# Sixteen more exponential tiles on VectorE, with a second FFN activation buffer, FFN and output tiles spread over the span, and the last shift of these tiles done in place

## The chip, the cores and the metric

One core of a Trainium2 chip. The metric is the device time of one execution in microseconds, the median of several. All executions compared here are of the fast state. Ratios are the mean time of one kernel's fast runs over that of the other's in the same rounds, so they are not quite the ratio of the medians quoted beside them.

## The reference, cut to what matters

```python
xn = layernorm(x)                       # x: 2048 x 512
q, k, v = xn @ wq, xn @ wk, xn @ wv     # 32 query heads of 16, one key/value head
p = softmax(q @ k.T * 16 ** -0.5)       # 32 heads x 2048 x 2048 scores
attn = (p @ v) @ wo
ffn = gelu(xn @ w1 + b1) @ w2 + b2      # 1792 hidden columns, tanh form of gelu
return x + attn + ffn
```

Almost everything hangs on the 32 x 2048 x 2048 exponentials. They are cut into 2048 tiles of 128 keys by 512 queries of one head.

## The kernel before: the parts concerned

The kernel records every operation with its dependencies, and a list scheduler inside it fixes the order on each engine. ScalarE (ACT) does exponentials; VectorE (DVE) takes some tiles off it, the **D tiles**: an approximate exponential by integer arithmetic on the bit pattern, in five shifted versions, each multiplied with its own scaled V on PE. A string, `DTAB`, says for each unit of three tiles whether tile 0 or tile 2 is a D tile (`.`: none).

```python
def exp(u):                                   # one ACT instruction for the 2 or 3 other tiles
    exps.append(act(lambda e: e.activation(E[:, s0:s0 + na, :], bank(b0, na)..., ACT.Exp, ...)))
    for i, t in enumerate(ts):
        if is_d[t]: p1(t, 3 * x + i)

def p1(t, bk):                                # D tile, first step: out of PSUM
    dve(lambda e: e.tensor_scalar(Dt[:, KZ, s, :], bank(bk), ..., ALU.add, ALU.max), ...)

def close_batch():                            # up to KB = 3 D tiles
    for k in order:
        if k != KZ:                           # four shifts, each into a version of its own
            dve(lambda e, k=k: e.tensor_scalar(Dt[:, k, s0:s0 + n, :], Dt[:, KZ, s0:s0 + n, :],
                                               float(SPL_K[k]), None, ALU.add), ...)
        for t, s in batch:
            pv_mm(gg, j, 1 + k, kt, Dt[:, k, s, :].bitcast(bf), [("D", s, k)])
```

`Dt` has 5 versions of a ring of 8 slots. Beside this run, per block of 512 rows: 14 hidden tiles of the FFN (matmuls, eviction by DVE, GELU arithmetic on DVE with a tanh on ACT) into **one** buffer `ub`, and four output tiles that read `ub`. Where they stand in the stream of 683 units is set by constants: the output tiles of the previous block at units 3, 12, 21 and 30 of a block, its own hidden tiles from 40 to 165.

Of the kernel before, what the change touches and what calls it, by code (L numbers as in the profile page):

```python
# [10 lines left out]
P = 128  # L11
# [27 lines left out]
NE_ND_KB = (25, 8, 3)  # L39
LA = 34  # L40
LB = 105
LY = 9
LP = 121
LS = 107
# [6 lines left out]
DTAB = "...00.20.0022.00.2...202202.22..0.200220..220..0.02.222002.20...2200220.2.0.2220.0...200000..002002.2.00..200220..00.200.0000....02.220.22.0220.02...2.22200022.0.2..220..20200220.20.20.220....22.200.2222.020020...2220.222.0222.0.020......2.2..0..020202....0220.20..0022.02.0...22..2220.2020.22.20...0.020020002...0020...02.00..0002202.022....222.2222.2222.0000..222.0.0222.022.200....00000.2020.00.02.2...22202.2.22.0000.000...2.2200.22..22.20.0...2.2.2.002..020020....220.2200.002.22.000....000020.2200.22200...02202.2.2002..2022...222220..0.2222.0020..22.00002.02.222020....20222...0202..0..2...220....2000.2.0.22....2.2.2.00..2.002020...0.00.2202.02000.00...20022.02.00.202000...."  # L51
# [7 lines left out]
YS = 9  # L59
HA = 40  # L60
HB = 165
# [365 lines left out]
def bass_parallel_sum__grouped_kv_mqa__dense_activation_gelu__prompt_kernel(  # L427
# [27 lines left out]
    NPR = 5  # L455
    NV = 1 + len(SPL_K)
    KZ = SPL_K.index(0)
    GAM = 128.0 / LN2 * 0.25
# [3 lines left out]
    with ExitStack() as es:  # L462
# [4 lines left out]
        ub = sb([P, FT, TBW], bf, "ub")  # L467
        xn = ub[:, 0:8, :]
        xnT = sb([P, DT, S], bf, "xnT")
        wvk = sb([P, DT, 2 * Dh], bf, "wvk")  # L470
        wkp = sb([P, DT, 4, 32], bf, "wkp")
        wq_sb = sb([P, DT, D], bf, "wq_sb")
        wqp = sb([P, DT, HG, 32], bf, "wqp")
# [31 lines left out]
        scr = sb([P, D], bf, "scr")  # L505
# [4 lines left out]
        ksq = sb([P, NT, Dh], f32, "ksq")  # L510
# [5 lines left out]
        Vf = sb([P, NT, Dh], f32, "Vf")  # L516
# [6 lines left out]
        Dt = sb([P, len(SPL_K), ND, TBW], i16, "Dt")  # L523
# [7 lines left out]
        oTp = sb([P, NPR, TBW], bf, "oTp")  # L531
# [41 lines left out]
        def dma(eng, o, i, stream, r=(), w=(), lat=2.2, allow=1.0, **kw):  # L573
            return add(eng, lambda e: e.dma_start(o, i), r, w, dma=stream, occ=0.7, lat=lat, allow=allow, **kw)
# [29 lines left out]
        dve(lambda e: e.memset(wkp[:], 0.0), w=["wkp"], n=256, due=0.0)  # L604
        dve(lambda e: e.memset(wqp[:], 0.0), w=["wqp"], n=512, due=0.1)
# [14 lines left out]
        for v, c in enumerate((1.0,) + SPL_C):  # L620
            setup(lambda e, v=v, c=c: e.memset(V1[:, v, :, Dh:Dh + 1], c), r=["V1"], w=["V1"], due=11.0)
        setup(lambda e: e.memset(sel8[:], 0.0), w=["sel8"], occ=0.3, due=12.0)
# [16 lines left out]
        def ln_batch(ts, how):  # L639
# [4 lines left out]
            if how == "a":  # L644
                for ti in ts:
                    act(lambda e, ti=ti: e.activation(scr[:], x_sb[:, ti, :], ACT.Identity, accum_out=sm[:, ti:ti + 1]),
                        r=[("x", ti)], w=["scr", ("sm", ti)], n=TBW + 250, due=land(ti))
                setup(lambda e: e.tensor_scalar(mean[:, sl], sm[:, sl], 1.0 / D, None, ALU.mult),
                      r=[("sm", ti) for ti in ts], w=mk, occ=0.2)
                setup(lambda e: e.tensor_scalar(nm[:, sl], sm[:, sl], -1.0 / D, None, ALU.mult),  # L650
                      r=[("sm", ti) for ti in ts], w=[("nm", ti) for ti in ts], occ=0.2)
                for ti in ts:
                    act(lambda e, ti=ti: e.activation(scr[:], x_sb[:, ti, :], ACT.Square, bias=nm[:, ti:ti + 1],
                                                      accum_out=sm[:, ti:ti + 1]),
                        r=[("x", ti), ("nm", ti)], w=["scr", ("sm", ti)], n=TBW + 250, due=land(ti))
                setup(lambda e: e.tensor_scalar(ve_b[:, sl], sm[:, sl], 1.0 / D, 1e-5, ALU.mult, ALU.add),
                      r=[("sm", ti) for ti in ts], w=[("ve", b)], occ=0.2)
            else:
                for ti in ts:
                    dve(lambda e, ti=ti: e.bn_stats(stats[:, ti, :], x_sb[:, ti, :]), r=[("x", ti)], w=[("st", ti)],  # L660
                        n=530, due=land(ti) + 1.0)
# [32 lines left out]
        def normed(ti):  # L694
            b, mean_ap = batch_of[ti]
            if XN_ENG[ti] == "d":
                dve(lambda e: e.tensor_scalar(xn[:, ti % 8, :], x_sb[:, ti, :], mean_ap, rstd[:, ti:ti + 1], ALU.subtract, ALU.mult),  # L697
                    r=[("x", ti), ("rstd", b), ("mv", b, ti)], w=[("u", ti % 8)], n=270, due=land(ti) + 2.0)
            else:
                act(lambda e: e.activation(xn[:, ti % 8, :], x_sb[:, ti, :], ACT.Identity, bias=nmr[:, ti:ti + 1],  # L700
                                           scale=rstd[:, ti:ti + 1]),
                    r=[("x", ti), ("rstd", b), ("nmr", b)], w=[("u", ti % 8)], n=TBW + 60, due=land(ti) + 2.0)

        def x_T(ts, bk, eng):
# [5 lines left out]
            for k, ti in enumerate(ts):  # L710
                for d in range(DT):
                    o = (d * n + k) * P
                    add("pe", lambda e, ti=ti, d=d, o=o: e.transpose(pT[:, o:o + P], xn[:, ti % 8, d * P:(d + 1) * P], ident[:]),  # L713
                        r=[("u", ti % 8), "ident"], w=[B(bk)], occ=0.085, due=land(ti) + 3.0)
# [95 lines left out]
        for v, c in enumerate(SPL_C):  # L810
            setup(lambda e, v=v, c=c: e.tensor_scalar(V1[:, 1 + v, :, 0:Dh], Vf[:], c, None, ALU.mult),
# [69 lines left out]
        def p1(t, bk):  # L881
            if not batch and dptr[0] + KB > ND:
# [4 lines left out]
            dve(lambda e: e.tensor_scalar(Dt[:, KZ, s, :], bank(bk), float(127 * 128) + SPL_D, SPL_MIN, ALU.add, ALU.max),  # L887
                w=[B(bk), ("D", s, KZ)], allow=P1_ALLOW, kind="p1")
# [7 lines left out]
        def close_batch():  # L896
            n = len(batch)
            s0 = batch[0][1]
            order = [KZ] + [k for k in range(len(SPL_K)) if k != KZ]
            for k in order:  # L900
                if k != KZ:
                    dve(lambda e, k=k: e.tensor_scalar(Dt[:, k, s0:s0 + n, :], Dt[:, KZ, s0:s0 + n, :], float(SPL_K[k]),  # L902
                                                       None, ALU.add),
                        r=[("D", s0 + i, KZ) for i in range(n)], w=[("D", s0 + i, k) for i in range(n)],
                        n=n * TBW, mode=4, allow=1.0, kind="post")
                for t, s in batch:
                    gg, kt, j = tile_of(t)
                    pv_mm(gg, j, 1 + k, kt, Dt[:, k, s, :].bitcast(bf), [("D", s, k)])
            del batch[:]

        onorm = {}

        def o_evac(gg):
# [20 lines left out]
            if h or end:  # L934
# [3 lines left out]
                                                r=keys, w=[("oTp", sl)], allow=3.0)  # L938
# [54 lines left out]

        def h_mm(tb, ft, ev=EV_ALLOW):
# [6 lines left out]
        def h_chain(tb, fts, al=3.0):  # L1001
# [3 lines left out]
            uu = ub[:, f0:f0 + n, :]  # L1005
            hk = [("h", s0 + i) for i in range(n)]
            uk = [("u", f) for f in fts]
# [8 lines left out]
        def y_mm(tb, i, start=True, stop=False, bk=7, fts=range(FT), al=1.5):  # L1016
            for ft in fts:
                mm4(bank(bk), ub[:, ft, i * P:(i + 1) * P], w2_sb[:, ft, :], start and ft == fts[0], stop and ft == fts[-1],
                   r=[("u", ft), "w2"], w=[B(bk)], allow=al)

        def wo_mm(tb, i, ps, start=False, bk=7, al=1.5):
            for n, p in enumerate(ps):
                pp = tb * NGR // 2 + p
                hs = [h for h in range(2) if 2 * pp + h < NTB * NGR - 1]
                assert all(2 * pp + h in onorm for h in hs)
# [6 lines left out]
        def store(tb, i):  # L1032
            ti = tb * 4 + i
            dma("sp", of[ti * P:(ti + 1) * P, :], x_sb[:, ti, :], f"d_o{i}", r=[("x", ti)], w=[("ob", i)])

        def out_tile(tb, i):
# [3 lines left out]
            ti = tb * 4 + i  # L1040
            dve(lambda e: e.tensor_tensor(x_sb[:, ti, :], pM, x_sb[:, ti, :], ALU.add), w=[("x", ti)] + M4, allow=EV_ALLOW)
            store(tb, i)

        xpy = x_sb[:, 0:8, :].rearrange("p t d -> p (t d)").bitcast(f32).rearrange("p (t d) -> p t d", d=D)

        def y_tile(tb, i):
            ti = tb * 4 + i
            y_mm(tb, i, al=YT_ALLOW[i])
            wo_mm(tb, i, range(FIN_G), al=YT_ALLOW[i])
            b2_mm(stop=i < 3, al=YT_ALLOW[i])  # L1050
            if i < 3:
                dve(lambda e: e.tensor_tensor(xpy[:, i, :], pM, x_sb[:, ti, :], ALU.add), r=[("x", ti)],
                    w=M4 + [("x", 2 * i), ("x", 2 * i + 1)], allow=EV_ALLOW)
            else:
                mm4(pM, ident, x_sb[:, ti, :], False, False, r=["ident", ("x", ti)], w=[B(7)], allow=YT_ALLOW[i])
# [22 lines left out]
        for tb in range(NTB):  # L1078
            u0 = tb * UPT
            if tb > 0:  # L1080
                for i in range(4):
                    at(u0 + 3 + (YS if tb < NTB - 1 else 9) * i, lambda tb=tb, i=i: out_tile(tb - 1, i), 0.6)
                q_at(tb, 3, u0 + Q3, (2, 3), (4, 5, 6, 7))
            a, b = (HA, HB) if tb < NTB - 1 else (LA, LB)
            if tb == 0:
                a = 18
            nf = FT if tb < NTB - 1 else FT - FIN_F
            for f0 in range(0, nf, 3):
                fts = list(range(f0, min(nf, f0 + 3)))
                for ft in fts:  # L1090
                    at(u0 + a + (b - a) * ft / FT, lambda tb=tb, ft=ft: h_mm(tb, ft), 0.6)
                at(u0 + a + (b - a) * fts[-1] / FT, lambda tb=tb, fts=fts: h_chain(tb, fts), len(fts) * 1.067 + 0.33)
# [3 lines left out]
            else:  # L1096
                for i in range(4):
                    at(u0 + LS + LY * i, lambda tb=tb, i=i: y_tile(tb, i), 0.6)
                fts = list(range(nf, FT))
                for ft in fts:  # L1100
                    at(u0 + LP + ft - nf, lambda tb=tb, ft=ft: h_mm(tb, ft), 0.6)
                if fts:
                    at(u0 + LP + len(fts), lambda tb=tb, fts=fts: h_chain(tb, fts, LAL), (len(fts) * 1.067 + 0.33) * LCO)
# [66 lines left out]
        for i in (0, 1, 3, 2):  # L1170
            ti = tb * 4 + i
            w = [(B(FB[i]), j) for j in range(4)] + ([B(FB[i])] if i < 3 else []) + [("x", ti)]
            if i < 3:
                dve(lambda e, i=i, ti=ti: e.tensor_tensor(x_sb[:, ti, :], bank(FB[i]), xpy[:, i, :], ALU.add),
                    r=[("x", 2 * i), ("x", 2 * i + 1)], w=w)
            else:
                act(lambda e, i=i, ti=ti: e.activation(x_sb[:, ti, :], bank(FB[i]), ACT.Copy), w=w)
            store(tb, i)
# [44 lines left out]
```

## Time and profile before

| | before |
|---|---|
| time, median | 797.58 us (796.94 to 798.07) |
| busy: PE, DVE, ACT | 767.0, 739.8, 774.0 us of a span of 795.8 |
| D tiles | 439 |
| start of first exponential, of last, end | 30.00, 785.36, 795.81 us |

The lines behind it stand in the prediction, with the measure that is used throughout: for ACT, the distance between the starts of successive instructions. 0.903 us for a two-tile and 1.330 for a three-tile exponential (medians in this trace: 0.904 and 1.330) are taken as the price without a wait; what is over that is called late, although the profile counts part of it as busy.

### The profile page before, as it was taken

How to read it: one execution, taken by the hardware profiler on the slowest of the kernel's cores; microseconds unless marked ns; L12 is line 12 of the kernel's file. 1: busy time of each engine (PE TensorE's matmuls, PEld its weight loads, DVE VectorE, ACT ScalarE, POOL GpSimd, SP SyncE). 2: the span in 40 equal slices, each digit the busy share in tenths (PEclk: the TensorE clock that was granted, in tenths of full speed). 3: DMA queues.
4: the chain of work that ended last, by engine and by line, in shares of the span. 5: the costliest groups of instructions: out<-in, count | busy, mean ns of one | idle time of the engine just before them, and what ended most of it. 6: DMA issues, size and time to landing. Idle time of an engine off the chain costs nothing.

```text
span 795.8 us, 20778 instructions
## 1 busy us (share of the span) xinstructions
PE 767.0 (96%) x8759; PEld 240.5 (30%) x8759; DVE 739.8 (93%) x1401; ACT 774.0 (97%) x734; POOL 20.8 (3%) x84
## 2 busy tenths in 40 slices
PE   6799999999999999999999999999999999999998
PEld 4323322232222323322232233322233233323222
DVE  8589999999998959999999889999999998999896
ACT  4899999999999999999999999999999999999995
POOL 6300000000000000000000000000000000000000
PEclk7899999999999999999999999999999999999999
DMA  9101100000000010001000001100001010000001
GB/s 312 41 9 30 23 15 16 17 21 13 12 22 23 23 29 16 17 15 22 17 13 24 20 19 23 22 16 16 19 12 22 24 22 23 16 9 16 16 9 35
DMA packets 30007, 21.17 MB, mean 27 GB/s; under 512 B 16353, under 2 KB 25434, under 8 KB 29914
## 3 DMA queue, kind: packets, MB, share of 16 engines
q1 hardware_dynamic: 28330, 19.28, 9.4%
q8 instruction: 69, 1.13, 0.6%
q10 hardware_dynamic: 1584, 0.56, 0.3%
q14 instruction: 24, 0.20, 0.1%
HBM read 10.98 MB, written 2.35 MB: 17 GB/s over the span
## 4 chain that ended last, share of the span: by engine, by line
ACT 92%; PE 5%; DVE 3%; DMA 0%; issue 0%; DVEq 0%
ACT E L870 88%; ACT ub L1012 3%; PE pAll L891 2%; PE pAll L851 1%; DVE stats L660 1%; PE pAll L567 1%; PE pAll L561 1%; DVE Dt L887 0%; DVE Dt L902 0%; DMA x_sb<-in_A_x_dram 0%; ACT xnT L718 0%; PE pAll L713 0%; ACT KT L732 0%; ACT ub L700 0%; DVE ub L697 0%
## 5 line engine op out<-in xcount | busy, mean ns | idle before, releaser
L870 ACT ACTIVATE E<-pAll 128x1024 bf16<-128x1024 f32 (+1 forms) x683 | 736.7, 1335 | 1.5 <-PE pAll L851 1.3
L891 PE MATMUL pAll<-Dt,V 128*32 128x512 bf16 x2195 | 390.0, 383 | 0.3
L887 DVE TENSOR_SCALAR Dt<-pAll 128x512 int16<-128x512 f32 x439 | 292.9, 680 | 28.9 <-PE pAll L851 28.3
L891 PE MATMUL pAll<-E,V 128*32 128x512 bf16 x1609 | 303.2, 387 | 1.4 <-DVE Of L915 1.2
L902 DVE TENSOR_SCALAR Dt<-Dt 128x1536 int16<-128x1536 int16 (+1 forms) x608 | 297.6, 533 | 0.9
L851 PE MATMUL pAll<-QT,KT 32*128 32x512 bf16 x2048 | 268.3, 386 | 15.0 <-ACT E L870 8.4
L851 PEld LDWEIGHTS pAll<-QT,KT 32*128 32x128 bf16 x2048 | 68.8, 91 | 290.4 <-ACT E L870 222.9
L891 PEld LDWEIGHTS pAll<-Dt,V 128*32 128x32 bf16 x2195 | 105.6, 94 | 107.0 <-issue 54.8
L567 PE MATMUL pAll<-xnT,w_sb 128*32 128x512 bf16 x896 | 128.1, 382 | 0.1
L567 PE MATMUL pAll<-w_sb,ub 128*32 128x512 bf16 x896 | 125.4, 382 | 0.0
L891 PEld LDWEIGHTS pAll<-E,V 128*32 128x32 bf16 x1609 | 70.7, 93 | 77.0 <-issue 59.1
L567 PE MATMUL pAll<-wop,oTp 128*32 128x512 bf16 x256 | 50.8, 381 | 0.0
L998 DVE TENSOR_SCALAR hb<-pAll,b1T 128x512 bf16<-128x512 f32 x56 | 41.5, 740 | 0.8 <-PE pAll L891 0.5
L567 PEld LDWEIGHTS pAll<-xnT,w_sb 128*32 128x32 bf16 x896 | 33.6, 95 | 24.1 <-issue 10.0
L567 PEld LDWEIGHTS pAll<-w_sb,ub 128*32 128x32 bf16 x896 | 32.1, 95 | 11.8 <-issue 5.2
L1184 PE MATMUL pAll<-xnT,zeros 128*32 128x512 bf16 x308 | 33.1, 383 | 0.0
L1012 ACT ACTIVATE ub<-ub 128x1536 bf16<-128x1536 bf16 (+1 forms) x20 | 32.1, 1606 | 0.0
L915 DVE COPY Of<-pAll 128x512 f32<-128x512 f32 x31 | 21.1, 680 | 5.0 <-PE pAll L567 4.1
L567 PE MATMUL pAll<-xnT,wq_sb 128*32 128x512 bf16 x256 | 20.5, 398 | 0.0
L1011 DVE TENSOR_TENSOR ub<-ub,hb 128x1536 bf16<-128x1536 bf16 (+1 forms) x20 | 17.9, 893 | 0.1
L1014 DVE TENSOR_TENSOR ub<-ub,hb 128x1536 bf16<-128x1536 bf16 (+1 forms) x20 | 17.9, 894 | 0.1
L1009 DVE TENSOR_TENSOR ub<-hb 128x1536 bf16<-128x1536 bf16 (+1 forms) x20 | 17.8, 892 | 0.1
(124 smaller groups left out, 242.7 us busy)
## 6 DMA issues: line engine op xcount, KB each, us to landing
OfP<-Of SPq DMA_DIRECT2D x124, 32.0 KB, 1.9
rbP<-rden_rows SPq DMA_DIRECT2D x124, 32.0 KB, 1.8
w_sb<-in_B_w_dram SPq DMA_DIRECT2D x2, 1792.0 KB, 13.5
x_sb<-in_A_x_dram SPq DMA_DIRECT2D x8, 256.0 KB, 6.1
out_dram<-x_sb SPq DMA_DIRECT2D x16, 128.0 KB, 1.7
QT<-qp SPq DMA_DIRECT2D x124, 16.0 KB, 1.8
wq_sb<-in_A_wq_dram ACTq DMA_DIRECT2D x1, 512.0 KB, 6.5
wop<-in_A_wo_dram SPq DMA_DIRECT2D x1, 512.0 KB, 16.3
```

The lines of the kernel that those rows point to most:

```text
L567: add("pe", lambda e, c=c, j=j: e.matmul(o[c, :], l[:, c], rh, start=start, stop=stop, tile_position=(0, 32 * j)), r, [(k, j) for k in w] ...
L851: ins = e.matmul(o, l, rh, start=True, stop=True, tile_position=(q0, 0))
L870: exps.append(act(lambda e: e.activation(E[:, s0:s0 + na, :], bank(b0, na).rearrange("p (a n) -> p a n", a=na), ACT.Exp, scale=LN2 / 128.0 ...
L887: dve(lambda e: e.tensor_scalar(Dt[:, KZ, s, :], bank(bk), float(127 * 128) + SPL_D, SPL_MIN, ALU.add, ALU.max), w=[B(bk), ("D", s, KZ)], ...
L891: add("pe", lambda e, a, b: e.matmul(pO[32 * j:32 * j + 32, :], V1[:, v, kt, :], rhs, start=a, stop=b, tile_position=(0, 32 * j)), r=r + [ ...
L902: dve(lambda e, k=k: e.tensor_scalar(Dt[:, k, s0:s0 + n, :], Dt[:, KZ, s0:s0 + n, :], float(SPL_K[k]), None, ALU.add), r=[("D", s0 + i, KZ ...
L915: dve(lambda e: e.tensor_copy(Of[:, i, :], pO), w=["O", ("Of", i)], allow=0.0)
L998: dve(lambda e: e.tensor_scalar(hb[:, ft % 6, :], pM, b1T[:, ft:ft + 1], None, ALU.add), r=["b1T"], w=M4 + [("h", ft % 6)], allow=ev)
L1011: dve(lambda e: e.tensor_tensor(uu, uu, hh, ALU.mult), r=uk + hk, w=uk, n=c, mode=2, allow=al)
L1012: act(lambda e: e.activation(uu, uu, ACT.Tanh, scale=GELU_K), r=uk, w=uk, n=c, allow=al - 0.5, kind="tanh")
L1014: dve(lambda e: e.tensor_tensor(uu, uu, hh, ALU.mult), r=uk + hk, w=uk, n=c, mode=2, allow=al)
L1184: pr.filler = lambda e, j, o: e.matmul((pO if o else pM)[32 * j:32 * j + 32, :], zeros[:, 0:32], xnT[:, 0, 0:TBW], start=not o, stop=not o ...
```

## The change

The intent is to give ACT fewer tiles and DVE more, which needs an evener load on DVE. Three parts make the room, and the fourth uses it:

- a second FFN activation buffer, laid over `x` (blocks alternate between `ub` and `x_sb`; the x rows that an output tile adds are loaded again from HBM);
- hidden and output tiles placed by two explicit lists that overlap;
- the last shift of a batch written over its first version, so that four versions suffice and the ring can be 12 instead of 8 (setup scratch moves into `oTp` for room);
- a new `DTAB` with 455 D tiles instead of 439.

Two small sizes change with them: the ring of exponentials `E` goes from 25 to 23 tile slots, and `oTp` from 5 to 6.

```diff
-NE_ND_KB = (25, 8, 3)
+NE_ND_KB = (23,12,3)
-DTAB = "...00.20.0022.00.2...202202.22..0.200220. [cut] "     # 439
+DTAB = "....0.2022200.2200...20.02002.20.02.0000. [cut] "     # 455
-YS = 9
-HA = 40
-HB = 165
+HP = ((18,160),(180,320),(330,470),(480,590))                       # hidden tiles, in units
+YP = ((174,213,252,291),(345,384,423,462),(516,537,558,579),(600,620,640,647))   # output tiles
+        ubs = (ub, x_sb)
-        Dt = sb([P, len(SPL_K), ND, TBW], i16, "Dt")
+        Dt = sb([P, len(SPL_K) - 1, ND, TBW], i16, "Dt")
 [cut: close_batch]
+                elif step:                                  # last shift
+                    b = 0
+                        dve(lambda e, k=k: e.tensor_scalar(Dt[:, 0, s0:s0 + n, :], Dt[:, 0, s0:s0 + n, :], ...
 [cut]
-            uu = ub[:, f0:f0 + n, :]
+            uu = ubs[tb % 2][:, f0:f0 + n, :]
+        def x_load(tb, i):
+            dma("sp", x_sb[:, 14 + i % 2, :], x_view[:, ti, :], ...)
```

## The prediction

> **What bounds the kernel now.** I read the page's busy shares first, then the chain that ended last, then the groups of instructions, then stretches of 100 us.
>
> ```profile
> PE 767.0 (96%) x8759; PEld 240.5 (30%) x8759; DVE 739.8 (93%) x1401; ACT 774.0 (97%) x734; POOL 20.8 (3%) x84
> ...
> ACT 92%; PE 5%; DVE 3%; DMA 0%; issue 0%; DVEq 0%
> ...
> L870 ACT ACTIVATE E<-pAll 128x1024 bf16<-128x1024 f32 (+1 forms) x683 | 736.7, 1335 | 1.5 <-PE pAll L851 1.3
> L887 DVE TENSOR_SCALAR Dt<-pAll 128x512 int16<-128x512 f32 x439 | 292.9, 680 | 28.9 <-PE pAll L851 28.3
> ```
>
> Three engines are over 90% busy, so the shares alone decide nothing. The chain decides: 92% of the span is ScalarE (ACT), and the exponentials waited only 1.5 us in all. VectorE (DVE) had 28.9 us of idle before the D tiles' first instruction, waiting for scores to appear: it was ahead of the others, not behind.
>
> The 2048 score tiles are handled three to a unit, 683 units. In each unit ACT exponentiates two or three tiles; the third may be a "D tile" that DVE turns into an approximate exponential by integer arithmetic (one step out of PSUM, then four shifts in SBUF on batches of up to three, each followed by a multiplication with V). The same groups with forms kept apart:
>
> ```profile
> L870 ACT ACTIVATE E<-pAll 128x1024 bf16<-128x1024 f32 x440 | 447.3, 1189 | 0.8 <-PE pAll L851 0.6
> L870 ACT ACTIVATE E<-pAll 128x1536 bf16<-128x1536 f32 x243 | 364.3, 1599 | 0.7 <-PE pAll L851 0.7
> L902 DVE TENSOR_SCALAR Dt<-Dt 128x1536 int16<-128x1536 int16 x548 | 277.4, 548 | 0.9
> L902 DVE TENSOR_SCALAR Dt<-Dt 128x1024 int16<-128x1024 int16 x52 | 18.9, 415 | 0.0
> L902 DVE TENSOR_SCALAR Dt<-Dt 128x512 int16<-128x512 int16 x8 | 1.8, 279 | 0.0
> ```
>
> The busy sums (447.3 + 364.3 = 811.6) exceed the 736.7 of the union, so consecutive instructions overlap and the mean duration is not the price. The price is the distance between successive starts in the trace. Its medians: two-tile exponential 0.904 us, three-tile 1.330, wide tanh 1.373; on DVE, D tile's first step 0.601, shift of three tiles 0.468, of two 0.335, of one 0.202. At undisturbed prices (0.903 and 1.330) the exponentials need 440 x 0.903 + 243 x 1.330 = 720.5 us. The starts before the next instruction sum to 733.4; about 3 us of the excess is the wait after the very last one, so ACT loses about 10 us of some 755 (from first exponential at 30.0 to last at 785.4). **ACT is full; only less work on it shortens the kernel.** Outside that stretch lie 30 us of prologue and 10.4 us of tail.
>
> ```profile
> 200.00:300.00 100.00, 98.64 (x1204) 29.46 (x1203) 87.95 (x169) 100.00 (x94) 0.00 (x0) 1.00 0.09 21
> 300.00:400.00 100.00, 98.49 (x1055) 30.13 (x1054) 98.86 (x185) 100.00 (x94) 0.00 (x0) 1.00 0.08 17
> 400.00:500.00 100.00, 99.47 (x1211) 30.29 (x1211) 92.21 (x179) 100.00 (x95) 0.00 (x0) 1.00 0.08 20
> 500.00:600.00 100.00, 97.39 (x1056) 29.48 (x1054) 99.01 (x180) 99.40 (x93) 0.00 (x0) 1.00 0.07 17
> ```
>
> Columns: stretch, then PE, PEld, DVE, ACT, POOL busy, granted clock, DMA share, GB/s. DVE alternates between 88 to 92% and 99%. The low stretches are where the output tiles of one block of 512 rows are computed (1211 matmuls against 1055) and no FFN activation is; the high ones are where the FFN hidden tiles and their GELU arithmetic run. There is one activation buffer, so a block's hidden tiles cannot be written until the previous block's output tiles have read theirs.
>
> **What the Trainium skill says.** "Perfetto Trace Analysis", section Optimizing Scalar/DVE Operations, puts ACT's busy overhead at about 51 ns with a PSUM operand and 93 ns on SBUF, and says the profiled latency is longer because its acknowledgement overlaps the next instruction. The trace agrees: 1024 elements at the 1.2 GHz of "ScalarE: Activation LUTs", Specifications, are 853 ns, plus 51 is 904; tanh on SBUF 1280 + 93 = 1373. For DVE the page gives 125 ns on PSUM; the trace's 601 ns less 512/0.96 GHz = 533 leaves only 68, so I use the trace. "VectorE: DVE Perf Modes", The perf-mode tier table, lets a 16-bit tensor_scalar in SBUF run at 4x; 1536/4/0.96 = 400, measured 468: agrees, and an in-place shift, with equal shapes and types, should cost the same. "Perfetto Trace Analysis", Optimization Strategy, recommends interleaving regimes with different limits, which is the intent here.
>
> **The change part by part.** I counted the instructions of both programs in their scheduled order.
>
> *D tiles moved from ACT to DVE: 439 becomes 455.* Two-tile exponentials go 440 to 456, three-tile 243 to 227. ACT: 16 x (1.330 - 0.903) = **-6.8 us**, all on the path. Tanh count and size are unchanged (16 wide, 4 narrow).
>
> *DVE gains.* First steps +16 x 0.60 = 9.6. Shifts of three tiles 548 to 564, +16 x 0.467 = 7.5; of two 52 to 48, -1.3; of one 8 to 32, +4.9 (161 batches for 152, with more small ones at group ends). Sum **+20.6 us**, beside ACT's work if it fits.
>
> *Does it fit?* At these prices (0.60 for other 512-column steps, 0.66 for hidden tile evictions, 0.866 and 0.466 for the wide GELU steps) DVE's work from the first D tile on is 706.6 us before and 726.6 after; ACT's exponentials and tanh are 746.3 before and 739.4 after. DVE over ACT: 94.7% to 98.3%. Cut in sixteen parts of 43 units, DVE/ACT was 79% at worst and 104% at most before; after, apart from the first part, it lies between 93 and 104%, and the running surplus never exceeds a few us. That evenness is what the second buffer and the spread of FFN and output tiles buy; by themselves they remove nothing from ACT.
>
> *PE.* Five multiplications for a D tile instead of one: 64 more. The trace starts these 32-row matmuls about 0.054 us apart when the four column groups are filled (estimate: 16 in a 0.86 us piece of the chain), so +3.5 us. But filler matmuls, which only occupy PE's gaps, fall from 308 to 212, so -5.2. PE keeps a small margin.
>
> *DMA.* The second buffer lies over x, so 16 reloads of x (128 KB each) are added, six units (some 6 us) before use. The stores of equal size land in 1.7 us at a DMA share of 7 to 10%. Zero on the path.
>
> *In-place last shift, ring of 12.* It frees one of five versions (5 x 8 = 40 tile slots become 4 x 12 = 48), and four full batches instead of two may be in flight. The new cost is a dependency: the in-place shift must wait until PE has read the unshifted tiles. In the scheduled order only 3 of 161 in-place shifts directly follow their own third shift; the median has 2.5 us of other DVE work between them, and 6.9 us since the batch's last first step. Estimate 0 to 3 us on DVE.
>
> *Sum.* 797.7 - 6.8 = 790.9. The trace's two-tile exponentials lose 28 ns each on average, the three-tile ones 2, so 16 more add 0.4. For a DVE without slack I add 0.3: **791.6**.
>
> **Rivals.** (a) *DVE becomes the bound.* Slack of 12.8 us at prices, plus ACT's own 10 us of losses, against DVE waits that were not mere slack: 5.0 us for finished attention sums, 3.9 for output tiles, perhaps 5 of the 28.9 before first steps. That is 14 of 23 us: fits, narrowly. Were half the 28.9 unavoidable, the end would come near 795. Against it: in 300 to 400 us DVE was already at 98.86% and ACT lost 1.0 us; in 200 to 300, with DVE at 87.95%, it lost 1.6. A full DVE did not slow ACT.
> (b) *The in-place shift waits on PE.* 161 batches by 0.2 us would be 32 us on DVE, more than its slack, and give about 800. The order of instructions speaks against it.
> (c) *Spreading the bursts removes ACT losses too.* If the 10 us of losses fell by a third, about 788. The losses are spread evenly (0.1 to 0.4 in nearly every 20 us), which looks like jitter of two-tile units, so I give it little.
> (d) *PE becomes the bound* where output tiles now share the stretch with hidden tiles: 798. The clock was 1.00 throughout and fillers remain.
>
> **Range and chances.** The floor is near 787 and needs (c) as well; (a) and (b) push up. Range 789 to 796. Faster by 2% would be below 781.8, twice the ACT saving: 0.01. Slower by 2% is above 813.7, needing a systematic stall: 0.02.
>
> **What would show it.** Right: 456 and 227 exponentials at 0.903 and 1.330 between starts, chain still about 92% ACT, DVE near 760 us busy (96%), its idle before first steps far below 28.9, an even DVE row, no wait on the reloads. Wrong: two-tile exponentials with a mean well above 0.93, a large DVE idle before the in-place shift, or scores waiting for DVE to free PSUM (29.2 us before).

## The result, and the profile after

789.04 us (788.29 to 790.68, four runs) against 797.58: 8.5 us less, ratio 0.9896 with a 95% interval of 0.9877 to 0.9915. It is a clear gain of 1%.

The page of the changed kernel, the lines that answer to those of the prediction (busy, the chain by engine, the two groups):

```profile
PE 759.7 (97%) x8727; PEld 235.3 (30%) x8727; DVE 756.6 (96%) x1453; ACT 767.0 (97%) x734; POOL 20.6 (3%) x84
...
ACT 96%; DVE 2%; PE 1%; DMA 0%; issue 0%; DVEq 0%
...
L883 ACT ACTIVATE E<-pAll 128x1024 bf16<-128x1024 f32 (+1 forms) x683 | 729.4, 1342 | 0.4 <-PE pAll L864 0.4
...
L900 DVE TENSOR_SCALAR Dt<-pAll 128x512 int16<-128x512 f32 x455 | 304.9, 681 | 8.1 <-PE pAll L864 7.2
```

ACT's share of the chain went up, from 92 to 96%, and PE's fell from 5 to 1%: that is a kernel closer to its one bound. DVE's idle before the D tiles' first step fell from 28.9 to 8.1 us; its spare time has been spent.

The forms of the exponential apart, and the shifts, of which L926 is the one in place:

```profile
L883 ACT ACTIVATE E<-pAll 128x1024 bf16<-128x1024 f32 x456 | 459.7, 1204 | 0.0
L883 ACT ACTIVATE E<-pAll 128x1536 bf16<-128x1536 f32 x227 | 339.9, 1619 | 0.4 <-PE pAll L864 0.4
...
L917 DVE TENSOR_SCALAR Dt<-Dt 128x1536 int16<-128x1536 int16 x423 | 218.2, 549 | 0.3
L926 DVE TENSOR_SCALAR Dt<-Dt 128x1536 int16<-128x1536 int16 x141 | 75.3, 544 | 0.2
```

The in-place shift cost DVE 0.2 us of waiting in all, and it is as fast as the others. The same stretches of 100 us (PE, PEld, DVE, ACT, POOL busy, clock, DMA share, GB/s):

```profile
200.00:300.00 100.00, 98.71 (x1157) 29.24 (x1152) 98.32 (x192) 100.00 (x97) 0.00 (x0) 1.00 0.09 23
300.00:400.00 100.00, 98.36 (x1125) 30.26 (x1123) 98.77 (x189) 100.00 (x95) 0.00 (x0) 1.00 0.09 22
400.00:500.00 100.00, 98.68 (x1151) 30.09 (x1146) 99.66 (x195) 100.00 (x95) 0.00 (x0) 1.00 0.09 21
500.00:600.00 100.00, 98.79 (x1137) 29.25 (x1132) 99.44 (x188) 100.00 (x96) 0.00 (x0) 1.00 0.10 22
```

DVE, 88 and 99% in turn before, is now at 98 to 100% throughout, and PE's matmuls are even too (1125 to 1157 per stretch, before 1055 to 1211). The 16 reloads of x landed in 2.1 us, and no engine's wait after the prologue names them.

Where the 9.2 us between the two profiled executions lie, from the starts of the first and the last exponential:

| us | before | changed | difference |
|---|---|---|---|
| start of the first exponential | 30.00 | 29.69 | -0.30 |
| first to last exponential | 755.36 | 747.37 | -7.99 |
| last exponential to the end | 10.45 | 9.55 | -0.90 |

The first line is less than what a repeat of the same kernel moves (0.48 us, below). The middle line is 1.2 us more than the 6.8 us that 16 cheaper units give, and the last line was not foreseen at all. The experiments had to explain both, and to show which parts of the change were needed.

### The profile page after: what moved, and what is told of

It reads as the page before. It is cut to its first block, busy times and chain, and to the rows that moved or that the text cites. A ratio compares the mean times of both kernels' runs of the same rounds, so it can differ in the third digit from the quotient of the medians.

```text
span 786.6 us, 20791 instructions
## 1 busy us (share of the span) xinstructions
PE 759.7 (97%) x8727; PEld 235.3 (30%) x8727; DVE 756.6 (96%) x1453; ACT 767.0 (97%) x734; POOL 20.6 (3%) x84
## 4 chain that ended last, share of the span: by engine, by line
ACT 96%; DVE 2%; PE 1%; DMA 0%; issue 0%; DVEq 0%
ACT E L883 92%; ACT ub L1038 2%; ACT x_sb L1038 2%; DVE stats L673 1%; PE pAll L570 1%; DMA x_sb<-in_A_x_dram 0%; ACT xnT L731 0%; PE pAll L726 0%; ACT KT L745 0%; ACT ub L713 0%; DVE ub L710 0%; DVE ub L1198 0%; DVE QT L772 0%; PE pAll L904 0%; PE pAll L576 0%
## 5 line engine op out<-in xcount | busy, mean ns | idle before, releaser
L883 ACT ACTIVATE E<-pAll 128x1024 bf16<-128x1024 f32 (+1 forms) x683 | 729.4, 1342 | 0.4 <-PE pAll L864 0.4
L904 PE MATMUL pAll<-Dt,V 128*32 128x512 bf16 x2275 | 388.6, 383 | 0.3
L900 DVE TENSOR_SCALAR Dt<-pAll 128x512 int16<-128x512 f32 x455 | 304.9, 681 | 8.1 <-PE pAll L864 7.2
L904 PE MATMUL pAll<-E,V 128*32 128x512 bf16 x1593 | 295.0, 387 | 0.8 <-DVE Of L938 0.3
L917 DVE TENSOR_SCALAR Dt<-Dt 128x1536 int16<-128x1536 int16 (+2 forms) x483 | 236.3, 526 | 0.3
L904 PEld LDWEIGHTS pAll<-Dt,V 128*32 128x32 bf16 x2275 | 103.9, 94 | 109.7 <-issue 58.7
L576 PE MATMUL pAll<-xnT,w_sb 128*32 128x512 bf16 x896 | 110.5, 382 | 0.2
L904 PEld LDWEIGHTS pAll<-E,V 128*32 128x32 bf16 x1593 | 68.7, 93 | 71.6 <-issue 55.4
L926 DVE TENSOR_SCALAR Dt<-Dt 128x1536 int16<-128x1536 int16 (+2 forms) x161 | 81.7, 521 | 0.2
L576 PE MATMUL pAll<-w_sb,ub 128*32 128x512 bf16 x448 | 58.6, 381 | 0.0
L576 PE MATMUL pAll<-w_sb,x_sb 128*32 128x512 bf16 x448 | 55.2, 382 | 0.0
L576 PE MATMUL pAll<-wop,oTp 128*32 128x512 bf16 x256 | 51.8, 382 | 0.0
L576 PEld LDWEIGHTS pAll<-xnT,w_sb 128*32 128x32 bf16 x896 | 29.0, 95 | 21.5 <-issue 10.9
L1208 PE MATMUL pAll<-xnT,zeros 128*32 128x512 bf16 x212 | 23.8, 383 | 0.0
L576 PE MATMUL pAll<-xnT,wq_sb 128*32 128x512 bf16 x256 | 20.8, 398 | 0.0
L576 PE MATMUL pAll<-b2row,ones 128*32 128x512 bf16 x64 | 18.6, 381 | 0.0
L576 PEld LDWEIGHTS pAll<-w_sb,ub 128*32 128x32 bf16 x448 | 17.0, 95 | 5.0 <-issue 1.6
```

The costliest lines, as they stand in the source:

```text
L576: add("pe", lambda e, c=c, j=j: e.matmul(o[c, :], l[:, c], rh, start=start, stop=stop, tile_position=(0, 32 * j)), r, [(k, j) for k in w] ...
L900: dve(lambda e: e.tensor_scalar(Dt[:, 0, s, :], bank(bk), float(127 * 128) + SPL_D, SPL_MIN, ALU.add, ALU.max), w=[B(bk), (("D", s), 0)], ...
L904: add("pe", lambda e, a, b: e.matmul(pO[32 * j:32 * j + 32, :], V1[:, v, kt, :], rhs, start=a, stop=b, tile_position=(0, 32 * j)), r=r + [ ...
L917: dve(lambda e, k=k, b=b: e.tensor_scalar(Dt[:, b, s0:s0 + n, :], Dt[:, 0, s0:s0 + n, :], float(SPL_K[k]), None, ALU.add), r=[(q, 0) for q ...
L926: dve(lambda e, k=k: e.tensor_scalar(Dt[:, 0, s0:s0 + n, :], Dt[:, 0, s0:s0 + n, :], float(SPL_K[k]), None, ALU.add), w=[(q, 0) for q in k ...
L1208: pr.filler = lambda e, j, o: e.matmul((pO if o else pM)[32 * j:32 * j + 32, :], zeros[:, 0:32], xnT[:, 0, 0:TBW], start=not o, stop=not o ...
```

## The experiments

All outputs are right. "Stretch" is the time from first to last exponential, "tail" what follows, both from the profiled execution. The changed kernel run again (a neighbour for the others) shows how steady these are: stretch 747.38 against 747.37, tail 9.56 against 9.55, while the first exponential moved by 0.48 us. So, as far as one repeat shows, stretch and tail can be read to a few hundredths, and the prologue's variation must be kept out of comparisons. (It can leak into the stretch: one run below waited 2.1 us just behind an early first exponential.)

| kernel | D tiles | time, us | ratio to before | stretch | tail |
|---|---|---|---|---|---|
| before (profile of 797.54) | 439 | 797.58 | 1 | 755.36 | 10.45 |
| changed | 455 | 789.04 | 0.9896 | 747.37 | 9.55 |
| changed again | 455 | 789.80 | 0.9899 | 747.38 | 9.56 |
| old D table in changed kernel | 439 | 801.50 | 1.0038 | 760.45 | 9.77 |
| new D table in old kernel | 455 | 833.71 | 1.0446 | 783.86 | 18.00 |
| old placing in changed kernel | 455 | 829.59 | 1.0399 | 777.73 | 22.58 |
| old placing and old table | 439 | 808.56 | 1.0132 | 756.64 | 20.80 |
| last output tiles back | 455 | 791.10 | 0.9911 | 749.58 | 11.30 |
| 16 D tiles fewer, table fitted | 439 | 795.35 | 0.9967 | 754.32 | 9.45 |
| 8 D tiles more, table fitted | 463 | 791.78 | 0.9925 | 748.10 | 11.28 |
| 3 D tiles more, table fitted | 458 | 788.07 | 0.9878 | 746.26 | 9.52 |
| five versions, ring of 9 | 455 | 797.90 | 1.0000 | 754.81 | 10.94 |
| in place, ring of 9 | 455 | 824.52 | 1.0328 | 784.04 | 10.09 |
| in place, ring of 6 | 455 | 873.47 | 1.0942 | 832.40 | 10.11 |

The theory: the gain is the swap of 16 tiles from ACT to DVE; buffer, spread and ring earn nothing by themselves, they make the room for it. The main rival: spreading the bursts removes waits of ACT, and that is the gain.

### The neighbour

No edit.

> The changed kernel once more, unaltered, as the neighbour of the runs of this call: 789.0 us; shows how far the ratio and the profiled parts (start of the first exponential, last exponential, end) move from one look to another.

789.80 us (788.87 to 790.23). The ratio moved from 0.9896 to 0.9899.

### First try: the old D table in the changed kernel

```diff
-DTAB = (455 D tiles, new)
+DTAB = (439 D tiles, of the kernel before)
```

> Everything of the changed kernel, but the 439 D tiles of the kernel before in their old places. Theory (the swap of 16 tiles from ScalarE to VectorE is the gain, the spread only makes room for it): ScalarE's work is back at 746.3 us from 739.4, so 789.0 + 6.8 = 795.8 us, still 1 to 2 us under the kernel before because the cleaner end stays. Rival (the spread itself removes waits and is most of the gain): 789 to 792 us.

801.50 us: slower than both kernels, and outside what either theory allowed. The stretch has two exponentials that started 1.83 and 2.09 us late, at 610.9 and 616.2 us, and four smaller waits (0.4 to 0.7 us), 5.95 us together. The old table puts D tiles thickly where, in the old placing, no hidden tiles ran; counted in the order of instructions, DVE had 105% of ACT's time in units 473 to 515, just before the two late ones (units 522 and 525). So this run could not tell the theories apart: the number of D tiles and how they fit the placing changed together. It showed that table and placing belong together.

### Second try: 439 D tiles in a table that fits

16 D tiles were taken out of the new table and the rest shifted by trial, with the kernel's own scheduler as guide, until no stretch was crowded.

```diff
-DTAB = (455 D tiles)
+DTAB = (439 D tiles, fitted to the new placing)
```

> The changed kernel with 439 D tiles instead of 455, taken out of its own table and the rest shifted a little so that no stretch is over 104% (VectorE over ScalarE). ScalarE's work 746.3 us, VectorE's 707.2. Theory (the swap of 16 tiles is the gain; with a table that fits the spread no stall is added): 789.0 + 6.8 = 795.8 us, 794.5 to 797. Rival (the spread itself, with fewer waits of ScalarE, is the gain): 789 to 791 us.

The exponentials of this run are again 440 and 243, and hardly wait:

```profile
L883 ACT ACTIVATE E<-pAll 128x1024 bf16<-128x1024 f32 x440 | 450.6, 1220 | 0.0
L883 ACT ACTIVATE E<-pAll 128x1536 bf16<-128x1536 f32 x243 | 366.5, 1642 | 0.7 <-PE pAll L864 0.7
```

795.35 us, 5.6 above the neighbour; the stretch is 754.32, so 754.32 - 747.38 = **6.94 us for 16 tiles**, where 16 x 0.427 = 6.83 had been predicted. (The time differs by less than the stretch does, because in the profiled pair this run's first exponential began 1.02 us earlier, at 29.16 against 30.18 us; why is open.) The rival's 789 to 791 is refuted. Against the kernel before, with as many D tiles, the stretch is 1.04 us shorter: that is what spread, buffer, ring and a table fitted to them earn in the stretch without the swap. In time they earn 2.5 us (797.89 to 795.35): the 1.04, another 1.0 in the tail (9.45 against 10.45), and the rest before the first exponential, where runs of one kernel differ by about as much. So of the 8.1 us of this call, 5.6 are the swap and 2.5 are not: the theory's "nothing by themselves" is not quite right.

The 1.04 us has an address. In the kernel before two exponentials inside the stretch began more than 0.3 us late: by 0.33 us at 421.6 and by 0.88 us at 590.6, 1.21 together. In this run and in the changed kernel none did. The second, in the timeline of the kernel before:

```profile
587.01 2.42 DVE L902 TENSOR_SCALAR Dt<-Dt 128x1536 int16<-128x1536 int16 x5
...
588.40 0.39 PE L851 MATMUL pAll<-QT,KT 32*128 32x512 bf16 x3
...
589.36 1.28 DVE L887 TENSOR_SCALAR Dt<-pAll 128x512 int16<-128x512 f32 x2
...
590.18 0.40 PE L851 MATMUL pAll<-QT,KT 32*128 32x512 bf16 x3
...
590.62 2.37 ACT L870 ACTIVATE E<-pAll 128x1024 bf16<-128x1024 f32 x2 [0.60 <-PE pAll L851]
```

DVE works off five shifts, then takes two D tiles out of PSUM late, those of units 506 and 507. ACT was done with unit 506 at 589.10 us, DVE only at 590.04; the scores of unit 508, which need its banks, begin at 590.18, 1.78 us after the last ones. ACT, waiting for them, stands idle 0.60 us; by the distance of starts, which leaves out the usual overlap, the exponential is 0.88 us late. It is in the part where hidden tiles had DVE at 104% of ACT's time. Without the two waits, the mean excess of a two-tile exponential over 0.903 us is (12.43 - 2.95 - 1.21) / 437 = 0.019 us before and (10.98 - 2.71) / 455 = 0.018 changed (2.95 and 2.71 follow the very last exponential): otherwise nothing changed on ACT.

### Is the room needed? The new table in the old kernel, and old placing in the new

```diff
 # kernel before
-DTAB = (439 D tiles, old)
+DTAB = (455 D tiles, new)
```

> The kernel before (one activation buffer, bursts, ring of 8, no in-place shift) with the 455 D tiles of the changed kernel in their new places. ScalarE's work is 739.4 us as in the changed kernel, VectorE's 726.6. Theory (room made by the spread is needed): in the stretches with hidden tiles VectorE has 105 to 111% of ScalarE's time, surpluses of some 4, 5 and 8 us, which ScalarE must wait out: 796 to 803 us, two-tile exponentials waiting for scores, whose banks VectorE frees late. Rival (only the number of D tiles counts): 789 to 791 us.

```diff
 # changed kernel
-HP = ((18,160),(180,320),(330,470),(480,590))
+HP = ((18,165),(210.75,335.75),(381.5,506.5),(546.25,617.25))
-YP = ((174,213,252,291),(345,384,423,462),(516,537,558,579),(600,620,640,647))
+YP = ((173.75,182.75,191.75,200.75), ...)      # nine units apart, as before
```

> The changed kernel with two activation buffers, in-place shift, ring of 12 and 455 D tiles, but hidden and output tiles at the places of the kernel before. Theory: a buffer that is not used to spread the work buys nothing, VectorE has 111, 112, 107 and 121% of ScalarE's time in the bursts: 796 to 805 us, near the run with the old kernel and 455 tiles. Rival (ring and buffers absorb the bursts): 789 to 792 us.

833.71 and 829.59 us: 36 and 32 us slower than the kernel before, where 5 and 7 at most had been expected. The direction is the theory's, the size was misjudged five- to sevenfold. The chain of the first of them, by engine, and its exponentials:

```profile
PE 40%; ACT 32%; DVE 25%; issue 2%; DMA 0%; DVEq 0%
...
L870 ACT ACTIVATE E<-pAll 128x1024 bf16<-128x1024 f32 (+1 forms) x683 | 732.0, 1231 | 29.4 <-PE pAll L851 27.5
...
L887 DVE TENSOR_SCALAR Dt<-pAll 128x512 int16<-128x512 f32 x455 | 305.3, 686 | 35.4 <-PE pAll L851 34.7
```

ACT stood idle 29.4 us before exponentials, 27.5 of it for scores, although it had no more work than in the changed kernel. The work on DVE is the same too. But DVE stood idle 35.4 us before first steps and was overfull elsewhere: time not used in one stretch is not fetched back in another. The code says why it cannot be: the scores of unit u + 2 go into the banks of unit u, so DVE may not fall behind by more than about two units. Units 506 and 508 above show it once; that it makes up the whole 36 us is argued, not measured. I had counted DVE's surplus over parts of 43 units, in which idle and overfull units cancel; at two units' reach they do not. In both runs the hidden tiles also came late: the last GELU product was at 800 and 808 us (712 in the changed kernel), which left output tiles for after the last exponential, tails of 18.0 and 22.6 us.

So a second buffer, the in-place shift and a deeper ring without the spread are worth 4 us of the 36 with 455 D tiles (829.6 for 833.7). The reverse, the spread with one buffer, was not run; the lists rule it out as they stand, since block 1's hidden tiles (from unit 180) are placed among block 0's output tiles (174 to 291). With the old table as well:

> The changed kernel's two buffers, in-place shift and ring of 12, with the placing of hidden and output tiles and the table of 439 D tiles of the kernel before. Theory (the parts that make room gain nothing until the room is used): not faster than the kernel before, 797 to 804 us. Rival (buffers or ring remove waits by themselves): 790 to 795 us.

```diff
 # changed kernel, HP and YP of the old placing as above
-DTAB = (455 D tiles, new)
+DTAB = (439 D tiles, old)
```

808.56 us, 10.7 above the kernel before and beyond the range I gave. The stretch is only 1.3 us longer (756.64), but the tail is 20.80 us: the last GELU product came at 770 us instead of 732, and output tiles followed the last exponential. Which of the remaining parts (in-place shift, the rings, second buffer) moved DVE's order so is not settled; no run separates them under the old placing. What is settled is that together they are no gain there.

### The tail: only the last block's output tiles moved back

```diff
-YP = (..., (600,620,640,647))
+YP = (..., (619.25,628.25,637.25,646.25))
```

> The changed kernel, only the four output tiles of the last block back at their later places (units 619 to 646 instead of 600 to 647). Theory (the end became 1.1 us shorter because PE no longer has output tile matmuls left over after the last exponential): matmuls of the last output tiles again after the last exponential, the end 0.5 to 1.2 us longer, 789.5 to 790.3 us. Rival (the end is shorter for another reason): 789.0 us and the same end.

791.10 us, above the range by 0.8. The tail is 11.30 us against 9.55 and 9.56. The stretch, 749.58, has 2.1 us of waits at 36 to 42 us, behind a prologue in which the first exponential began 0.8 us earlier than in the changed kernel; they are not a matter of output tiles. So the tail's 1.7 us is what this run shows. Its cause can be counted: matmuls with `w2` that start after the last exponential are 15 here, 1 before and none in the changed kernel, whose last one stands at 762.4 us, 14.7 us before the last exponential; in the kernel before the last was at 787.1 us, 1.8 us after it. Matmuls of the output projection for earlier heads, after the last exponential, are 39 here, 31 before and 20 in the changed kernel.

The chain of the kernel before shows the same, PE from 778 us on (a piece each for start, length, what):

```profile
784.93 0.33 PE pAll L891 x4
785.25 0.21 PE pAll L567
785.46 0.22 PE pAll L891 x4
...
787.08 0.87 PE pAll L567 x15
787.95 0.99 PE pAll L561 x8
788.93 0.76 PE pAll L567 x9
789.69 0.37 PE pAll L961 x2
790.06 0.32 PE pAll L567 x2
```

In the changed kernel the chain stays on ACT up to 777.4 us, past the start of the last exponential:

```profile
769.73 7.70 ACT E L883 x7
777.43 0.04 issue
777.48 0.40 PE pAll L904 x3
777.88 0.65 PE pAll L576 x12
...
778.86 0.43 DVE Of L967
```

L567 and L576 are the same helper's line in the two kernels; here its matmuls are those of the output projection, of the FFN and of the bias. Before, PE is behind: nine of the output projection (0.76 us) stand in front of the transposes of the last normalization (L961), and two of the bias (0.32 us) between them. After, PE waits for the last head group, and 0.65 us of output projection for earlier heads is all of it that is left on the chain.

### How far does the swap go? 8 and 3 D tiles more

```diff
-DTAB = (455 D tiles)
+DTAB = (463 D tiles; in the other run 458; each fitted in the same way)
```

> The changed kernel with 463 D tiles, the table again fitted. ScalarE's work 736.0 us (3.4 less), VectorE's 735.6 (9.0 more), so VectorE has no slack left in all but a few stretches. If ScalarE were still the only bound: 785.6 us. Theory (VectorE's slack, 12.8 us in the changed kernel, is what ends the gain): 789 to 795 us, ScalarE waiting for scores.

> The changed kernel with 458 D tiles, the table fitted: a candidate to beat it. ScalarE's work 738.2 us (1.2 to 1.3 less), VectorE's 730.5 (3.9 more). If ScalarE stays the bound: 787.8 us; if VectorE is the bound already: 789 to 791 us.

With 463 D tiles: 791.78 us. ACT has 3.4 us less to do and the stretch is 0.7 us longer. The chain shows what happened:

```profile
ACT 50%; DVE 26%; PE 21%; DMA 1%; issue 1%; DVEq 0%; ACTq 0%; POOL 0%
```

One exponential was late by 2.27 us, one by 1.05. This is the rival of the prediction in which DVE becomes the bound; it begins to come true eight tiles further on. The tail is 1.7 us longer too (11.28 against 9.56): the last GELU product came at 732.5 us instead of 712.8, and 24 matmuls with `w2` start after the last exponential. So more of the loss lies in the tail than in the stretch, and whether other places for the last tiles would save it was not tried.

With 458: 788.07 us (788.00 to 788.16), against 789.80 (788.87 to 790.23) of the changed kernel; ratios 0.9878 and 0.9899. No run of one overlaps one of the other, though the intervals of the ratios do (0.9865 to 0.9892, and 0.9885 to 0.9912). The stretch is 1.12 us shorter, of the 3 x 0.427 = 1.28 that the tiles are worth. It is a little faster than both kernels, and about where the swap ends.

### The in-place shift and the ring

```diff
 # five versions, ring of 9 (45 tile slots fit where 48 were)
-NE_ND_KB = (23,12,3)
+NE_ND_KB = (23,9,3)
-Dt = sb([P, len(SPL_K) - 1, ND, TBW], ...);  b = min(step, len(KORD) - 2);  if 0 < step < len(KORD) - 1:
+Dt = sb([P, len(SPL_K), ND, TBW], ...);      b = step;                      if 0 < step:
```

> The changed kernel with the last shift into a fifth version again, ring of 9 (45 tile slots, so that it fits where 48 were): three full batches instead of four, no waiting of a shift for PE. Theory (in-place shifting is there for the room, not for time): little lost, 790 to 796 us. Rival (the in-place shift waits on PE and costs time): below 789.

```diff
 # in place, ring of 9, and of 6
-NE_ND_KB = (23,12,3)
+NE_ND_KB = (23,9,3)
```

> The changed kernel with the in-place last shift and a ring of 9 instead of 12: differs from the run with five versions and a ring of 9 only in the in-place shift. Theory (in place, a slot's first version is held until the fifth multiplication has read it, so the next batch may start in it later; the deeper ring pays for that): clearly slower than with five versions, 800 to 825 us, VectorE idle before first steps or ScalarE late. Rival (a slot is free early enough, three batches are plenty): within 2 us of the run with five versions.

> In-place last shift with two full batches in flight, as many as the kernel before had in its ring of 8. By the same theory worse again, 840 to 900 us; rival: as the ring of 9.

797.90, 824.52 and 873.47 us, beside 789.0 for in place with a ring of 12. At the same ring of 9 the in-place shift costs 26.6 us; three slots more give back 35.5. So what pays is the room: 5 x 9 slots are slower than 4 x 12 in nearly the same memory by 8.9 us (7.4 in the stretch, 1.4 in the tail). The first of the three came out 1.9 us above my range. The table was fitted to a ring of 12 and not to these, so the numbers are prices at this table, not the best that each ring could do.

The reason expected was that an in-place slot is held until its fifth multiplication. The waits agree only in part. With a ring of 6:

```profile
L900 DVE TENSOR_SCALAR Dt<-pAll 128x512 int16<-128x512 f32 x455 | 302.3, 683 | 59.6 <-PE pAll L864 50.9 <-PE pAll L904 4.7 <-PE pAll L576 1.9
...
L926 DVE TENSOR_SCALAR Dt<-Dt 128x1536 int16<-128x1536 int16 (+2 forms) x161 | 81.5, 522 | 4.0 <-PE pAll L904 2.8
```

First steps waited 4.7 us, and in-place shifts 2.8, for the multiplications (L904), where the changed kernel names no such wait (0.2 us of idle before in-place shifts in all). With a ring of 9, which loses 26.6 us, they are only 0.4 and 0.2 us. Most of the wait is for scores (50.9 us): the order of instructions is fixed by the scheduler with the dependency in it, so the cost appears as scores and exponentials that come later. The size is shown, the way from the held slot to the late scores is argued.

## Why the prediction was right, point by point

**The swap: right.** 456 and 227 exponentials, -6.8 us predicted, -6.94 measured in the stretch between two kernels that differ in the D tiles alone; their times differ by 5.6 us (795.35 and 789.80), as the prologues differ.

**DVE's gains: right.** Its work was predicted at +20.6 us by distances of starts; its busy time, in which instructions overlap, rose by 16.8 to 756.6 us, 96% of the span, where the prediction had near 760 and 96%. It fitted: idle before first steps 8.1 instead of 28.9.

**PE and DMA: right.** Fillers 212 as counted, PE's share 97% after 96%, 2.1 us for a reload (some 6 us had been left for it), no wait for one.

**In-place shift: right for this ring.** 0.2 us of waiting, where 0 to 3 was allowed. What the prediction did not see is that the ring of 12 is the condition: at 9 slots the same shift loses 26.6 us.

**The added 0.7 us for losses: wrong in sign.** The prediction charged each two-tile exponential 28 ns, which had the final wait of 2.95 us and the two late exponentials in it; without those it is 19 ns, so 16 more add 0.3. And it read ACT's losses of the kernel before as even jitter that spreading could not touch ("I give it little"). Most of them are, but two late starts, of 0.33 and 0.88 us, were not, and went: -1.04 us. The larger one is traced to a DVE burst above. The prediction's own test, that a full DVE lost ACT no more in 300 to 400 us than a slack one in 200 to 300, looked at two stretches without such a start.

**The tail: a missing term.** The 10.4 us were taken as fixed. They held output tile matmuls that the new placing moves ahead of the last exponential: -0.90 us between the two profiles, and +1.7 when they are moved back.

With these two the sum is 797.6 - 6.9 - 1.0 - 0.9 = 788.8, against 789.04 measured and 791.6 predicted. The central number was 2.6 us high, and the result lies 0.04 us inside the lower edge of the range, while its own runs differ by 2.4 us: the mechanism was right, but that the number fell inside rather than just outside is luck.

**The rivals.** DVE as the bound: not at 455, but at 463 (791.78 us). PE as the bound: not in the stretch, and at the end it stopped being so. The rival in which spreading removes ACT's losses was right for 1 us of the 10.

## What to carry to other kernels

When two engines share divisible work and one of them is full, moving a unit of work earns its price on the full engine only while the other has room at that very place; room averaged over the span is not room, and 455 D tiles placed where they do not fit were 32 to 36 us slower than 439. So even out the second engine's other work first, then move units until the chain of waits leaves the full engine; and refit the table of moved units whenever buffers or places change. Look at the end by itself: side work that trails behind the last main instruction lengthens the kernel even where it is hidden everywhere else.

## What the Trainium skill lacked or had wrong

- "Perfetto Trace Analysis", section Optimizing Scalar/DVE Operations, gives DVE an overhead of about 125 ns with a PSUM operand. Here 455 instructions of 512 fp32 columns out of PSUM started 0.601 us apart in the median; less the 0.533 us that the prediction works out for 512 elements, that is 68 ns. Its 51 ns for ACT on PSUM fits to about 1 ns (medians of 0.904 and 1.330 us).
- "VectorE: DVE Perf Modes", The perf-mode tier table, puts a 16-bit tensor_scalar in SBUF at 4x, but neither it nor another page that I read says whether that holds with the output exactly over the input (a warning in the former is about outputs that overlap it in part). It does here, with the right result: 141 in-place shifts of 1536 elements and 423 into another buffer both started 0.468 us apart in the median.
- No page that I read has the excess of two-tile exponentials: 0.018 to 0.019 us on average over 0.903 where nothing is late by more than 0.3 us, against 0.002 us over 1.330 for three tiles (0.57 us over 227). Its cause is open.
